# Sums of exponentials by TensorE for two pairs of heads, and division of the values in place of the probabilities

## The chip, the cores and the metric

The kernel runs on one core of one Trainium2 chip. The metric is the device time of one execution in microseconds (us); 742.13 us is the median of three runs of the kernel before (741.7 to 743.33).

## What is computed

Attention over 4 batches, 8 heads, 768 positions and 64 columns a head, with a window of 96 keys, 8 global keys and a bias by distance, and then a gated projection of its 3072 rows.

```python
scores = q @ k.T / 8 + bias          # kept: own window of 96 keys, and the first 8
a = exp(scores - max(scores))
a = a / (sum(a) + 1e-9)
x = (a @ v), heads side by side      # 3072 x 512
out = ((x @ w_a) * (x @ w_b)) @ w_out   # 512 -> 1536 -> 512
```

All inputs are float32. The weights arrive as 64-bit words and are rebuilt as float32 in the kernel.

## The kernel before

The 24 blocks of 128 query rows are cut into eight units, of 4, 2 and six times 3 blocks (`UNITS`). The first unit's attention runs ahead; then, unit by unit, its projection (`moe`) runs beside the attention of the next one. A projection has twelve steps (`f`), each with 128 of the 1536 columns: two products of 512-row contraction into the banks p0 and p1 (`proj`, L984), their product on ScalarE and VectorE (`raw`, L415 and L1023), a split of it into a high and a low part (`hh`, `hl`), and three products for each block into `acc` (`back`, L1002). Every factor is split so (`xh`, `xl` and the halves of `wt`), three products for one. During the first unit's projection the weights are converted by ScalarE and VectorE (`load_w`, L451 to L425).

The first unit (`first`) handles heads in four pairs, c = 0 to 3. A pair has two quads, j = 0 and 1, each of two blocks (`quad`): scores of both heads (`scores`, L783, into the banks `ps`), and for each head and block one window of 128, 256 or 232 columns. `softmax` subtracts the bias and takes the minimum of the negated scores on VectorE (L613), takes the exponential on ScalarE with the sum in an accumulator that is read by an instruction of its own (L629), adds 1e-9 (L644), takes the reciprocal (L651), and multiplies the window by it on VectorE, GpSimd or ScalarE (L661, L663). `turn` transposes the probabilities on TensorE into one of the banks `pt` (L688) and copies them to `pf` (L415, L417). `values` multiplies them with v into the bank `pa` (L736): the first head of the pair into its partitions 0 to 63, the second into 64 to 127, in turn. Then `pa` is cast to `xh` and the rest goes to `xl` (L843).

Each engine's order is written out by a planner (`Schedule.order`): every operation has a due time, a cost on each engine that may do it, and its buffers; an engine takes the ready operation that is due first. `search` tries 400 sets of jittered due times for the operations of the first two units' time and keeps the one with the earliest end. So a change of any operation there can move every other one. On the chip an engine then works through its list in that order and waits for semaphores. The queue of the SyncE engine (SP) issues all loads in its own order.

Of the kernel before, what the change touches and what calls it, by code (L numbers as in the profile page):

```python
# [13 lines left out]
F32 = mybir.dt.float32  # L14
# [11 lines left out]
P = 128  # L26
# [5 lines left out]
G = 8  # L32
# [6 lines left out]

CHUNKS = 12  # L40
SQ = 32

SHORT = PAIRED
OLD = (0, 2, 3)
# [329 lines left out]
class Fast:  # L374
    def __init__(self, ctx, tc, qkv, wts, out, raw0, consts):
        self.tc, self.nc = tc, tc.nc
        self.qkv, self.wts, self.out = qkv, wts, out
        rel, col, self.sc, self.ident = consts
        self.ctx = ctx
        self.w = {}  # L380
        self.plan = Schedule()
        self.negd = self.plan.buf(None, None, F32, "negd", "negd", tile=rel)
        self.negd0 = self.plan.buf(None, None, F32, "negd0", "negd0", tile=col)


        self.raw0 = self.plan.buf(None, None, F32, "raw0", "raw0", tile=raw0)
# [216 lines left out]
            )  # L603
        return qh, ql, kk

    def softmax(self, h, due, wins, ps, t, sm, done=()):

        nc, op, n = self.nc, self.plan.op, len(wins)
        for j, (o, w) in enumerate(wins):
            neg = self.negd if w > P else self.negd0  # L610
            op(
                due,
                lambda e, j=j, o=o, w=w, neg=neg: nc.vector.tensor_tensor_reduce(  # L613
                    t[:, o : o + w],
                    ps[:, o : o + w],
                    neg[:, :w],
                    -(2.0 ** -(h + 1)),
                    3.0e38,
                    ALU.add,
                    ALU.min,  # L620
                    sm[:, j : j + 1],
                ),
                [ps, neg, *done],
                [(t, j), (sm, j)],
                dve=dve(w) + 10,
            )
# [29 lines left out]
        for j, (o, w) in enumerate(wins):  # L656

            def norm(e, j=j, o=o, w=w):
                r = sm[:, 3 * n + j : 3 * n + j + 1]
                if e == "act":  # L660
                    nc.scalar.mul(t[:, o : o + w], t[:, o : o + w], r)  # L661
                else:
                    self.engine(e).tensor_scalar(  # L663
                        t[:, o : o + w], t[:, o : o + w], r, 1.0, op0=ALU.mult, op1=ALU.mult
                    )

            op(
                due,
                norm,
                [(sm, "r")],  # L670
                [(t, j)],
                port=BOTH,
                dve=130 + 0.52 * w,
                pool=243 + 0.836 * w,
                act=act(w) + 100,
            )
# [45 lines left out]
                    dma=SWAP,  # L722
                )

    def values(self, due, pl, blocks, v, probs, pa):


        nc = self.nc

        def emit(e):  # L730
            for i in blocks:
                slots = pl.vslot[i]
                for c, slot in enumerate(slots):
# [12 lines left out]
        self.plan.op(due, emit, reads, [pa], pe=n * 218 + 290, spare=SPARE if pl.late else 0.0)  # L746

    def quad(self, u, c, j, due, raw, v, pa, homes):


        nc, pl, op, sp = self.nc, PLANS[u], self.plan.op, self.sbuf
# [41 lines left out]
        for s in range(2):  # L793
# [5 lines left out]
            self.softmax(2 * c + s, due, wins, ps[s], t, sm)  # L799
            pt = self.bank(pick("pt"), f"pt{s}_{n}")  # L800
            pf = t
            if homes["pf"]:
# [7 lines left out]
                o += len(pl.vslot[i]) * P  # L810
        if pa is None:
            pa = self.bank("psS", f"pa{n}")
        self.values(due, pl, blocks, v, probs, pa)
        return pa

    def first(self, end):
# [7 lines left out]
        homes = {  # L824
            "q": ("hl", WIDE),
            "s": (("psS", "acc0"), ("p0", "acc2")),
            "pt": ("psT", "p1", "acc1"),
            "t": (("kk", MAXK), ("raw", MAXC)),
            "pf": (("hh", WIDE), ("v", 2 * MAXV * D)),
        }  # L830
        loads = [self.fetch_first(c, -1e6 + 2 * c) for c in range(NCC)]
        step = end / NCC
        for c in range(NCC):
            pa = self.bank("psA", f"pa0_{c}")
            for j in range(2):
                self.quad(0, c, j, c * step + (j + 1) * step / 2, *loads[c], pa, homes)
# [4 lines left out]
            self.plan.op(  # L841
                due,
                lambda e, lo=get(lo, l0), hi=get(hi, h0), pa=get(pa): self.nc.vector.tensor_sub(  # L843
                    lo(), pa(), hi()
                ),
                [pa, (hi, c)],
                [(lo, -c - 1)],
                dve=dve(WIDE),
            )
        return xh, xl  # L850
# [495 lines left out]
    return sc  # L1346


def build_first(nc, cp, qkv, sc):

    pl = PLANS[0]
# [10 lines left out]
def build(nc, a, out):  # L1362
    with tile.TileContext(nc) as tc, ExitStack() as ctx:
        cp = ctx.enter_context(tc.tile_pool(name="c", bufs=1))
        with tc.manual_schedule(), tc.tile_pool(name="tmp", bufs=1) as tp:
# [7 lines left out]
            raw0 = build_first(nc, cp, a["qkv"], sc)  # L1373
            ident = cp.tile([P, P], F32, name="ident")
            make_identity(nc, ident)
            nf = build_counts(nc, cp, nv)
# [4 lines left out]
        main = Fast(inner, tc, a["qkv"], a["wts"], out, raw0, (rel, col, sc, ident))  # L1381
        with tc.If(fast > 0) as branch:
            with inner:
                main.run()
# [75 lines left out]
```

## Time and profile before

| | |
|---|---|
| profiled execution | 742.13 us, span of the trace 740.2 us |
| median of three runs | 742.13 us |
| TensorE (PE) busy | 717.2 us, 97% |
| VectorE (DVE) busy | 458.0 us, 62% |
| ScalarE (ACT) busy | 394.9 us, 53% |
| GpSimd (POOL) busy | 10.5 us, 1% |

The shares are means over a start, in which attention of the first unit runs alone, and a long rest, in which TensorE works on projections all the time. The chain that ended last passes through TensorE for 93% of the span. Times of an instruction overlap with those of its successor on the same engine, so what one costs its engine is read from start to start.

### The profile page before, as it was taken

To read this page: it belongs to the slowest core of one execution; us is meant where nothing else is said; L and a number is where in the kernel's file an instruction comes from. 1 tells how busy PE (TensorE), PEld (TensorE's weight loads), DVE (VectorE), ACT (ScalarE), POOL (GpSimd) and SP (SyncE) were. 2 spreads that over 40 slices of the span, in tenths; PEclk is the share of its full clock that TensorE was granted. 3 is DMA by queue.
4 is the path that set the end of the run, shared out by engine and by line. 5 is a ranking of instruction groups with operands and counts; after the bars stand their busy time and mean duration, and the time that the engine had idled before them with its cause. 6 is when DMAs were issued, how large, how long until landed. Compare 5 with 4: busy or idle time off the path is not lost.

```text
span 740.2 us, 12564 instructions
## 1 busy us (share of the span) xinstructions
PE 717.2 (97%) x4374; PEld 642.7 (87%) x4374; DVE 458.0 (62%) x1479; ACT 394.9 (53%) x984; POOL 10.5 (1%) x30
## 2 busy tenths in 40 slices
PE   5789999999999999999999999999999999999996
PEld 3567777789988999999999999999999999989995
DVE  6999999957646765376635776167653776321111
ACT  6999866557655554265635556155553656321112
POOL 1000000000000000000000001000000000000000
PEclk9999999999999999999999999999999999999999
DMA  7889111112322334223331243323242242210001
GB/s 282 321 335 366 64 32 32 49 67 80 88 85 88 90 100 106 67 66 99 87 111 65 79 128 99 82 69 104 78 121 66 78 121 61 57 49 1 0 1 47
DMA packets 36215, 72.61 MB, mean 98 GB/s; under 512 B 7728, under 2 KB 18736, under 8 KB 36144
## 3 DMA queue, kind: packets, MB, share of 16 engines
q1 hardware_dynamic: 36144, 71.73, 30.8%
q8 instruction: 36, 0.59, 0.3%
q14 instruction: 35, 0.29, 0.1%
HBM read 50.07 MB, written 6.29 MB: 76 GB/s over the span
## 4 chain that ended last, share of the span: by engine, by line
PE 93%; ACT 3%; DVE 3%; DMA 0%; issue 0%; ACTq 0%
PE p L984 54%; PE acc L1002 27%; PE pa L736 5%; PE ps L909 4%; PE pt L688 1%; PE ps L783 1%; ACT t L629 1%; ACT wr L494 1%; ACT pf L415 1%; DVE t L613 0%; DMA nv<-ns 0%; ACT wm L457 0%; DVE kk L425 0%; ACT t L661 0%; DVE t L663 0%
## 5 line engine op out<-in xcount | busy, mean ns | idle before, releaser
L984 PE MATMUL p<-xh,wt 128*128 128x384 f32 (+2 forms) x1488 | 421.1, 339 | 3.5 <-ACT raw L415 1.9
L984 PEld LDWEIGHTS p<-xh,wt 128*128 128x128 f32 x1488 | 271.8, 189 | 17.8 <-issue 3.7
L984 PE MATMUL p<-xl,wt 128*128 128x384 f32 (+2 forms) x816 | 270.2, 341 | 1.2 <-ACT xl L415 0.9
L1002 PE MATMUL acc<-wt,hh 128*128 128x512 f32 x576 | 203.4, 395 | 0.6 <-ACT hh L415 0.6
L984 PEld LDWEIGHTS p<-xl,wt 128*128 128x128 f32 x816 | 153.8, 189 | 10.5 <-ACT xl L415 1.2
L1023 DVE TENSOR_TENSOR raw<-p,raw 128x384 f32<-128x384 f32 (+2 forms) x96 | 53.2, 555 | 156.0 <-PE p L984 133.0
L1002 PEld LDWEIGHTS acc<-wt,hh 128*128 128x128 f32 x576 | 108.2, 188 | 21.4 <-issue 1.1
L1002 PE MATMUL acc<-wt,hl 128*128 128x512 f32 x288 | 113.2, 393 | 0.4 <-DVE hl L425 0.4
L415 ACT COPY raw<-p 128x384 f32<-128x384 f32 (+2 forms) x96 | 45.8, 477 | 114.0 <-PE p L984 113.7
L415 ACT CAST hh<-raw 128x384 fp32r<-128x384 f32 (+2 forms) x84 | 43.2, 514 | 49.6 <-DVE raw L1023 48.7
L425 DVE TENSOR_TENSOR hl<-raw,hh 128x384 fp32r<-128x384 f32 (+2 forms) x96 | 53.3, 556 | 24.8 <-ACT hh L415 24.2
L629 ACT ACTIVATE t<-t,sm 128x232 f32<-128x232 f32 (+2 forms) x120 | 56.9, 477 | 17.1 <-DVE sm L613 16.1
L1002 PEld LDWEIGHTS acc<-wt,hl 128*128 128x128 f32 x288 | 54.2, 188 | 8.3 <-DVE hl L425 0.7
L613 DVE CUSTOM_DVE_ANT_0 t<-ps,rel 128x232 f32<-128x232 f32 (+1 forms) x100 | 39.1, 400 | 28.2 <-PE ps L909 27.1
L661 ACT ACTIVATE t<-t,sm 128x232 f32<-128x232 f32 (+2 forms) x77 | 36.1, 479 | 18.7 <-DVE sm L651 14.9
L629 ACT ACTIVATE wm<-wm,sm 128x232 f32<-128x232 f32 (+2 forms) x72 | 34.1, 474 | 19.1 <-DVE sm L613 18.4
L661 ACT ACTIVATE wm<-wm,sm 128x232 f32<-128x232 f32 (+2 forms) x66 | 31.3, 478 | 21.0 <-DVE sm L651 13.6
L736 PE MATMUL pa<-pf,v 128*64 128x128 f32 x640 | 41.8, 277 | 0.6 <-PE pt L688 0.4
L736 PEld LDWEIGHTS pa<-pf,v 128*64 128x64 f32 x640 | 34.4, 137 | 8.4 <-issue 6.6
L425 DVE TENSOR_TENSOR kk<-raw,kk 64x244 fp32r<-64x244 f32 (+1 forms) x86 | 39.9, 464 | 2.6
L909 PE MATMUL ps<-kk,ql 128*128 128x128 f32 (+1 forms) x144 | 39.4, 275 | 0.0
L909 PE MATMUL ps<-kk,qh 128*128 128x128 f32 (+1 forms) x144 | 38.1, 267 | 0.0
(89 smaller groups left out, 666.7 us busy)
## 6 DMA issues: line engine op xcount, KB each, us to landing
wr<-wts SPq DMA_DIRECT2D x24, 768.0 KB, 12.0
pf<-wm SPq DMA_DIRECT2D x192, 48.0 KB, 1.9
raw<-qkv SPq DMA_DIRECT2D x24, 366.0 KB, 3.1
raw<-qkv SPq DMA_DIRECT2D x24, 314.0 KB, 2.9
v<-qkv SPq DMA_DIRECT2D x16, 384.0 KB, 3.5
out<-o SPq DMA_DIRECT2D x23, 256.0 KB, 2.1
pf<-wm SPq DMA_DIRECT2D x144, 40.0 KB, 1.9
v<-qkv SPq DMA_DIRECT2D x16, 256.0 KB, 2.8
```

Source lines behind the costliest of these rows:

```text
L415: self.nc.scalar.copy(out(), src())
L425: lambda e: self.engine(e).tensor_sub(out(), a(), b()),
L494: lambda e, low=low: nc.scalar.activation(low(), low().bitcast(U32), AF.Copy, scale=2.0**-29),
L613: lambda e, j=j, o=o, w=w, neg=neg: nc.vector.tensor_tensor_reduce(t[:, o : o + w], ps[:, o : o + w], neg[:, :w], -(2.0 ** -(h + 1)), 3.0e ...
L629: lambda e, j=j, o=o, w=w: nc.scalar.activation(t[:, o : o + w], t[:, o : o + w], AF.Exp, bias=sm[:, j : j + 1], scale=-1.0, accum_out=sm[ ...
L661: nc.scalar.mul(t[:, o : o + w], t[:, o : o + w], r)
L688: nc.tensor.transpose(pt[:, c * P : c * P + P], t[:, o : o + P], self.ident)
L736: nc.tensor.matmul(pa[D * s : D * s + D, i * P : i * P + P], v[:, v0 : v0 + D], probs[s, i][1](c), start=c == 0, stop=c == len(slots) - 1,)
L909: nc.tensor.matmul(ps[:, :w], q[:, i * P : i * P + P], kk[:, k0 : k0 + w], start=m == 0, stop=m == 1,)
L984: nc.tensor.matmul(p[:, :T], wt(), b[:, b0 : b0 + T], start=c == 0 and n == 0, stop=c == NCC - 1 and n == 2,)
L1002: nc.tensor.matmul(acc[i][:, :], hs[:, i * P : i * P + P], wt(), start=f == 0 and n == 0, stop=f == NF - 1 and n == 2,)
L1023: lambda e, asb=asb, pb=pb: nc.vector.tensor_mul(asb[:, :T], pb[:, :T], asb[:, :T]),
```

## The change

For the pairs c = 0 and 1 of the first unit (`SUMS`), `softmax` stops behind the exponential, which no longer has an accumulator. `values` gives TensorE, behind each product of v and probabilities, one of a matrix of ones (or of zeros and ones, where a slot holds fewer than 128 keys) and the same probabilities, into the same partitions of a bank `su`: every one of the 64 rows of a head gets the sums. ScalarE copies the sums plus 1e-9 to `y`, VectorE takes the reciprocal of all 512 columns and multiplies `pa` by it, and `xh` and `xl` are made of `y`. `su` lies in the bank acc1, which the transposed probabilities used as their third. GpSimd builds the matrix of ones at the start.

```diff
+SUMS = (0, 1)
-    def softmax(self, h, due, wins, ps, t, sm, done=()):
+    def softmax(self, h, due, wins, ps, t, sm, done=(), norm=True):
...
-                    accum_out=sm[:, n + j : n + j + 1],
+                    **({"accum_out": sm[:, n + j : n + j + 1]} if norm else {}),
...
-                act=act(w) + 200,
+                act=act(w) + (200 if norm else 100),
+        if not norm:
+            return
...
-    def values(self, due, pl, blocks, v, probs, pa):
+    def values(self, due, pl, blocks, v, probs, pa, sums=None):
...
+                        if sums:
+                            keys = len(pl.vkeys[slot][1])
+                            nc.tensor.matmul(
+                                sums[D * s : D * s + D, i * P : i * P + P],
+                                self.ones[:, :D] if keys == P else self.ones[:, D:],
+                                probs[s, i][1](c),
+                                start=c == 0,
+                                stop=c == len(slots) - 1,
+                            )
...
+        out = [pa, sums] if sums else [pa]
+        cost = len(out) * n * 218 + 290
...
-            "pt": ("psT", "p1", "acc1"),
+            "pt": ("psT", "p1"),
...
+            if c in SUMS:
+                sums = self.bank("acc1", f"su0_{c}")
...
+            y = pa
+            if sums:
+                y = sp([P, CHUNKS * P], F32, "pf", f"y0_{c}")
...
+                    lambda e, y=get(y), sums=get(sums): self.nc.scalar.activation(
+                        y(), sums(), AF.Identity, bias=self.tiny[:, 0:1]
+                    ),
...
+                    lambda e, y=get(y): self.nc.vector.reciprocal(y(), y()),
...
+                    lambda e, y=get(y), pa=get(pa): self.nc.vector.tensor_mul(y(), pa(), y()),
...
-            self.copy(due, get(hi, h0), get(pa), WIDE, [pa], [(hi, c)], psum=True)
+            self.copy(due, get(hi, h0), get(y), WIDE, [y], [(hi, c)], psum=sums is None)
...
-                    lo(), pa(), hi()
+                    lo(), y(), hi()
...
+def build_ones(nc, cp):
+    ones = cp.tile([P, 2 * D], F32, name="ones")
+    nc.gpsimd.iota(
+        ones, [[0, 2 * D]], base=0, channel_multiplier=1, allow_small_or_imprecise_dtypes=True
+    )
+    nc.gpsimd.tensor_scalar(ones, ones, float(P - LW - G), 0.0, op0=ALU.is_ge, op1=ALU.add)
+    nc.gpsimd.memset(ones[:, :D], 1.0)
+    tiny = cp.tile([P, 1], F32, name="tiny")
+    nc.gpsimd.memset(tiny, 1e-9)
```

The lists change with it. In names as `ps1_0_0_1` the first digit is the head of the pair, then unit, pair and quad. TensorE behind the first pair's scores, before:

```order
L688 MATMUL pt1_0_0_0_193<-ident_93,t1_0_0_0_162 128x128 x3
L688 MATMUL pt0_0_0_0_200<-ident_93,t0_0_0_0_157 128x128 x3
L783 MATMUL ps0_0_1_0_214<-raw0_1_160,qs0_1_0_207 128x128
L783 MATMUL ps1_0_1_0_216<-raw0_1_160,qs0_1_0_207 128x128
L783 MATMUL ps0_0_1_0_214<-raw0_1_160,qs0_1_0_207 128x256
L783 MATMUL ps1_0_1_0_216<-raw0_1_160,qs0_1_0_207 128x256
L688 MATMUL pt1_0_0_1_227<-ident_93,t1_0_0_1_173 128x128 x4
L783 MATMUL ps0_0_1_1_238<-raw0_1_160,qs0_1_1_222 128x232
```

and now, behind three transposes and the first two slots of values (L800 is the old L783, L693 the old L688, L742 the old L736, L751 the ones):

```order
L742 MATMUL pa0_0_210<-pf0_0_0_0_191,v0_0_155 64x128
L751 MATMUL su0_0_212<-pf0_0_0_0_191,ones_98 64x128
L742 MATMUL pa0_0_210<-pf1_0_0_0_207,v0_0_155 64x128
L751 MATMUL su0_0_212<-pf1_0_0_0_207,ones_98 64x128
L693 MATMUL pt1_0_0_1_232<-ident_93,t1_0_0_1_185 128x128 x4
L800 MATMUL ps0_0_1_0_239<-raw0_1_166,qs0_1_0_226 128x128
L800 MATMUL ps1_0_1_0_241<-raw0_1_166,qs0_1_0_226 128x128
L800 MATMUL ps0_0_1_0_239<-raw0_1_166,qs0_1_0_226 128x256
L800 MATMUL ps1_0_1_0_241<-raw0_1_166,qs0_1_0_226 128x256
L800 MATMUL ps0_0_1_1_247<-raw0_1_166,qs0_1_1_228 128x232
```

The values of the first quad, which stood behind the third pair's scores, now stand ahead of the second pair's, and each has a product with ones behind it.

VectorE where the second pair's windows end, before (L613 is a window with its minimum, with a row for the read of the minimum; L768 scales queries):

```order
L651 RECIPROCAL sm0_0_1_0_233<-sm0_0_1_0_233 128x2
L613 ISA t0_0_1_1_270,sm0_0_1_1_271<-ps0_0_1_1_238,rel_70 128x232
L613 ISA sm0_0_1_1_271 128x1
L663 TENSOR_SCALAR t0_0_1_0_232<-t0_0_1_0_232,sm0_0_1_0_233 128x256
L613 ISA t1_0_1_1_274,sm1_0_1_1_275<-ps1_0_1_1_240,rel_70 128x232
L613 ISA sm1_0_1_1_275 128x1
L644 TENSOR_SCALAR sm1_0_1_0_236<-sm1_0_1_0_236 128x2
L768 TENSOR_SCALAR qs0_3_0_289<-raw0_3_212,sc_79 128x256
L651 RECIPROCAL sm1_0_1_0_236<-sm1_0_1_0_236 128x2
L663 TENSOR_SCALAR t1_0_1_0_235<-t1_0_1_0_235,sm1_0_1_0_236 128x128
```

and now (L616 is the old L613, L785 the old L768, L873 the reciprocal and L881 the multiplication of `y`, L419 a cast):

```order
L785 TENSOR_SCALAR qs0_2_1_297<-raw0_2_200,sc_79 128x256
L873 RECIPROCAL y0_0_304<-y0_0_304 128x512
L616 ISA t0_0_2_0_330,sm0_0_2_0_331<-ps0_0_2_0_310,col_71 128x128
L616 ISA sm0_0_2_0_331 128x1
L881 TENSOR_TENSOR y0_0_304<-pa0_0_210,y0_0_304 128x512
L616 ISA t0_0_2_0_330,sm0_0_2_0_331<-ps0_0_2_0_310,rel_70 128x256
L616 ISA sm0_0_2_0_331 128x1
L419 CAST xh0_345<-y0_0_304 128x512
L616 ISA t1_0_2_0_363,sm1_0_2_0_364<-ps1_0_2_0_312,col_71 128x128
L616 ISA sm1_0_2_0_364 128x1
L616 ISA t1_0_2_0_363,sm1_0_2_0_364<-ps1_0_2_0_312,rel_70 128x256
```

The small adds and reciprocals and the normalizations are gone; the reciprocal of 512 columns stands ahead of the third pair's first window, and the multiplication and the cast of `y` between its windows.

ScalarE up to the copy of the first projection out of its bank, before (L494 and L457 convert weights):

```order
L494 ACTIVATE wr2_0_434<-wr2_0_434 128x768
L494 ACTIVATE wr2_1_459<-wr2_1_459 128x768
L457 ACTIVATE wm_440<-wr2_0_434 128x768
L415 CAST xl0_387<-pa0_3_592 128x512
L494 ACTIVATE wr3_0_488<-wr3_0_488 128x768
L494 ACTIVATE wr3_1_510<-wr3_1_510 128x768
L415 CAST wt1_0_654<-wm_440 128x768
L494 ACTIVATE wr4_1_557<-wr4_1_557 128x768
L415 COPY raw0_88<-p00_0_535 128x512
```

and now (L496, L459 and L417 are the old L494, L457 and L415):

```order
L417 COPY pf0_0_3_1_613<-pt0_0_3_1_603 128x512
L496 ACTIVATE wr1_1_366<-wr1_1_366 128x768
L496 ACTIVATE wr2_0_427<-wr2_0_427 128x768
L417 CAST wt1_0_638<-wm_398 128x768
L417 CAST xl0_370<-pa0_3_553 128x512
L459 ACTIVATE wm_398<-wr2_0_427 128x768
L496 ACTIVATE wr2_1_456<-wr2_1_456 128x768
L459 ACTIVATE wm_398<-wr2_1_456 128x768
L417 COPY raw0_88<-p00_0_572 128x512
```

Fewer weight conversions stand ahead of the copy (the last row of each), and those of the third step in another order.

## Rows read from the trace of the kernel before

**Rows 1.** The page's head and its busy time of each engine
```profile
span 740.2 us, 12564 instructions
...
PE 717.2 (97%) x4374; PEld 642.7 (87%) x4374; DVE 458.0 (62%) x1479; ACT 394.9 (53%) x984; POOL 10.5 (1%) x30
```

**Rows 2.** Stretches: busy us (instructions) of PE, PEld, DVE, ACT, POOL, TensorE clock, DMA
```profile
17.40:50.10 32.70, 25.34 (x214) 18.32 (x210) 31.93 (x111) 32.16 (x83) 0.00 (x0) 0.95 0.83 316
50.10:100.00 49.90, 49.87 (x250) 39.37 (x251) 49.70 (x96) 45.19 (x80) 0.00 (x0) 1.00 0.56 215
```

**Rows 3.** The chain of waits: start us, us, what
```profile
49.61 0.47 ACT raw L415
...
50.13 1.90 PE p L984 x7
```

**Rows 4.** Timeline, ScalarE: start us, us, instruction, [idle before <-releaser]
```profile
7.79 0.40 ACT L629 ACTIVATE t<-t,sm 128x128 f32<-128x128 f32 x1 [1.65 <-DVE sm L613]
...
18.23 0.47 ACT L629 ACTIVATE t<-t,sm 128x232 f32<-128x232 f32 x1
18.61 0.19 ACT L629 ACTIVATION_READ_ACCUMULATOR t<-t,sm 128x1 f32 x1
18.70 0.47 ACT L629 ACTIVATE t<-t,sm 128x232 f32<-128x232 f32 x1
...
22.57 0.58 ACT L415 CAST xh<-pa 128x512 fp32r<-128x512 f32 x1
23.04 1.09 ACT L415 COPY pf<-pt 128x512 f32<-128x512 f32 x2
```

**Rows 5.** Timeline, VectorE, 17 to 24 us
```profile
17.28 0.16 DVE L644 TENSOR_SCALAR sm<-sm 128x2 f32<-128x2 f32 x1
17.35 0.39 DVE L613 CUSTOM_DVE_ANT_0 t<-ps,rel 128x232 f32<-128x232 f32 x1
...
18.05 0.35 DVE L663 TENSOR_SCALAR t<-t,sm 128x256 f32<-128x256 f32 x1
18.31 0.39 DVE L613 CUSTOM_DVE_ANT_0 t<-ps,rel 128x232 f32<-128x232 f32 x1
...
20.51 0.16 DVE L651 RECIPROCAL sm<-sm 128x2 f32<-128x2 f32 x1
20.59 0.40 DVE L613 CUSTOM_DVE_ANT_0 t<-ps,rel 128x256 f32<-128x256 f32 x1
...
23.37 0.69 DVE L843 TENSOR_TENSOR xl<-pa,xh 128x512 fp32r<-128x512 f32 x1
23.97 0.39 DVE L613 CUSTOM_DVE_ANT_0 t<-ps,rel 128x232 f32<-128x232 f32 x1
```

**Rows 6.** Groups of VectorE instructions by shape: busy us, mean ns, idle before
```profile
L651 DVE RECIPROCAL sm<-sm 128x1 f32<-128x1 f32 x144 | 23.2, 161 | 3.9
...
L651 DVE RECIPROCAL sm<-sm 128x2 f32<-128x2 f32 x24 | 3.8, 160 | 0.1
```

**Rows 7.** Timeline, TensorE, the first 22 us
```profile
5.80 3.20 PE L783 MATMUL ps<-raw 64*128 64x128 f32 x16 [5.80 <-DVE rel L1335]
...
12.51 1.66 PE L783 MATMUL ps<-raw,qs 64*128 64x128 f32 x8
...
20.31 1.75 PE L736 MATMUL pa<-pf,v 128*64 128x128 f32 x28
21.99 1.42 PE L688 MATMUL pt<-ident,t 128*128 128x128 f32 x11
```

**Rows 8.** Stretches of 0.05 us, TensorE's instructions on pa: busy us (in flight), clock, DMA
```profile
20.30:20.35 0.05, 0.04 (x2) 1.00 1.46 614
...
20.45:20.50 0.05, 0.05 (x4) 1.00 0.58 246
```

**Rows 9.** Timeline, VectorE, at the sixth step
```profile
85.88 0.95 DVE L425 TENSOR_TENSOR wt<-wm,wt 128x768 fp32r<-128x768 f32 x1
```

**Rows 10.** Timeline, TensorE, at the sixth step
```profile
87.47 0.39 PE L984 MATMUL p<-xh,wt 128*128 128x512 f32 x1
```

More of the change, by code (lines that the diff above doesn't have):

```diff
@@ L377, in __init__ @@
         self.qkv, self.wts, self.out = qkv, wts, out
-        rel, col, self.sc, self.ident = consts
+        rel, col, self.sc, self.ident, self.ones, self.tiny = consts
         self.ctx = ctx
@@ L742, in emit, with quad @@
                         )
+                        if sums:
[7 more added lines that the diff above has]
+                            )
         reads = [v] + [probs[s, i][0] for s in range(2) for i in blocks]
         n = sum(len(pl.vslot[i]) for i in blocks)
-        self.plan.op(due, emit, reads, [pa], pe=n * 218 + 290, spare=SPARE if pl.late else 0.0)
-    def quad(self, u, c, j, due, raw, v, pa, homes):
+        out = [pa, sums] if sums else [pa]
+        cost = len(out) * n * 218 + 290
+        self.plan.op(due, emit, reads, out, pe=cost, spare=SPARE if pl.late else 0.0)
+    def quad(self, u, c, j, due, raw, v, pa, homes, sums=None):
         nc, pl, op, sp = self.nc, PLANS[u], self.plan.op, self.sbuf
@@ L798, in quad @@
             sm = sp([P, 8], F32, "sm", f"sm{s}_{n}", 6)
-            self.softmax(2 * c + s, due, wins, ps[s], t, sm)
+            self.softmax(2 * c + s, due, wins, ps[s], t, sm, norm=sums is None)
             pt = self.bank(pick("pt"), f"pt{s}_{n}")
@@ L812, in quad @@
             pa = self.bank("psS", f"pa{n}")
-        self.values(due, pl, blocks, v, probs, pa)
+        self.values(due, pl, blocks, v, probs, pa, sums)
         return pa
@@ L833, in first @@
         for c in range(NCC):
-            pa = self.bank("psA", f"pa0_{c}")
+            pa, sums = self.bank("psA", f"pa0_{c}"), None
+            if c in SUMS:
+                sums = self.bank("acc1", f"su0_{c}")
             for j in range(2):
-                self.quad(0, c, j, c * step + (j + 1) * step / 2, *loads[c], pa, homes)
+                self.quad(0, c, j, c * step + (j + 1) * step / 2, *loads[c], pa, homes, sums)
             (hi, h0), (lo, l0) = xh[c], xl[c]
@@ L839, in first @@
             due = (c + 1) * step
-            self.copy(due, get(hi, h0), get(pa), WIDE, [pa], [(hi, c)], psum=True)
+            y = pa
+            if sums:
+                y = sp([P, CHUNKS * P], F32, "pf", f"y0_{c}")
+                self.plan.op(
+                    due,
+                    lambda e, y=get(y), sums=get(sums): self.nc.scalar.activation(
+                        y(), sums(), AF.Identity, bias=self.tiny[:, 0:1]
+                    ),
+                    [sums],
+                    [y],
+                    act=act(WIDE, True),
+                )
+                self.plan.op(
+                    due,
+                    lambda e, y=get(y): self.nc.vector.reciprocal(y(), y()),
+                    [],
+                    [y],
+                    port=BOTH,
+                    dve=dve(WIDE),
+                )
+                self.plan.op(
+                    due,
+                    lambda e, y=get(y), pa=get(pa): self.nc.vector.tensor_mul(y(), pa(), y()),
+                    [pa],
+                    [y],
+                    dve=dve(WIDE),
+                )
+            self.copy(due, get(hi, h0), get(y), WIDE, [y], [(hi, c)], psum=sums is None)
             self.plan.op(
                 due,
-                lambda e, lo=get(lo, l0), hi=get(hi, h0), pa=get(pa): self.nc.vector.tensor_sub(
-                    lo(), pa(), hi()
+                lambda e, lo=get(lo, l0), hi=get(hi, h0), y=get(y): self.nc.vector.tensor_sub(
+                    lo(), y(), hi()
                 ),
-                [pa, (hi, c)],
+                [y, (hi, c)],
                 [(lo, -c - 1)],
+                port=BOTH if sums else (),
                 dve=dve(WIDE),
@@ L1346, in build_scales @@
     return sc
+def build_ones(nc, cp):
+    ones = cp.tile([P, 2 * D], F32, name="ones")
+    nc.gpsimd.iota(
+        ones, [[0, 2 * D]], base=0, channel_multiplier=1, allow_small_or_imprecise_dtypes=True
+    )
+    nc.gpsimd.tensor_scalar(ones, ones, float(P - LW - G), 0.0, op0=ALU.is_ge, op1=ALU.add)
+    nc.gpsimd.memset(ones[:, :D], 1.0)
+    tiny = cp.tile([P, 1], F32, name="tiny")
+    nc.gpsimd.memset(tiny, 1e-9)
+    return ones, tiny
 def build_first(nc, cp, qkv, sc):
@@ L1375, in build @@
             make_identity(nc, ident)
+            ones, tiny = build_ones(nc, cp)
             nf = build_counts(nc, cp, nv)
@@ L1380, in build @@
         inner = ctx.enter_context(ExitStack())
-        main = Fast(inner, tc, a["qkv"], a["wts"], out, raw0, (rel, col, sc, ident))
+        main = Fast(inner, tc, a["qkv"], a["wts"], out, raw0, (rel, col, sc, ident, ones, tiny))
         with tc.If(fast > 0) as branch:
```

## The prediction

> **What bounds the kernel now.** First the page's head and busy shares: TensorE is busy for 717.2 of 740.2 us, so the time is its work plus the little it stands still [rows 1]. Next the stretches: from 50.1 us on it hardly stands (49.87 of 49.90 us); what it loses, it loses ahead of that. In 17.4 to 50.1 VectorE is busy for 31.93 and ScalarE for 32.16 of 32.70 us, TensorE for 25.34 [rows 2]. I call the moment when TensorE begins the second of the twelve steps of the first projection the handover. The chain of waits shows what sets it: ScalarE works without a break through casts and weight conversions, copies the first projection out of its bank at 49.61, and TensorE begins at 50.13 [rows 3]. Ahead of the handover both programs give TensorE the same projection work (24 products of 512 columns), and behind it the same remainder. So the change is worth what it moves the handover, less what TensorE must wait behind it.
>
> **ScalarE up to that copy.** An exponential of 232 columns takes 0.38 us until its accumulator is read and 0.09 more until the next begins (18.23, 18.61, 18.70) [rows 4]; the change drops sixteen reads: 16 x 0.09 = 1.44. Two normalizations of the first two pairs stood here, of 232 and 128 columns: the 0.38 of such a pass and some 0.3, together 0.7. Added are two copies of sums at the 0.47 of a 512-column pass (22.57 to 23.04) [rows 4]: 0.94. The new order also moves work: a cast of x (0.47) and a copy of probabilities (0.36) go to VectorE, three scalings of queries come here (3 x 0.4), normalizations of later pairs cost 0.5 more, and two more weight conversions of 0.8 fall behind the copy. Sum: -1.44 - 0.7 + 0.94 - 0.83 + 1.2 + 0.5 - 1.6 = -1.9.
>
> **VectorE up to the last subtraction of x.** Removed: 8 adds and 8 reciprocals at 0.07 to 0.08, 1.2, and 14 normalizations, 0.26 for 256 columns (18.05 to 18.31) and a little less for the ten smaller ones, 3.4 [rows 5]. Added: two multiplications of 512 columns at the 0.60 of a subtraction of that size (23.37 to 23.97), 1.2 [rows 5], and two reciprocals of 512 columns, which no row shows. Their low end is the same 0.60. The high end comes from the small ones: a successor begins 0.08 behind a reciprocal (20.51, 20.59) and 0.07 behind an add (17.28, 17.35) [rows 5]; were that 0.01 the price of two columns, 5 ns each, 512 would cost 0.60 + 2.6 = 3.2. I take 0.60: 144 reciprocals of one column average 161 ns and 24 of two columns 160, so that the second column costs nothing visible [rows 6]. The moves add 0.8 (cast, copy) and take away 0.8 of query scalings and some normalizations, one of them to GpSimd. Sum about -3.4. The subtraction for these pairs reads SBUF now, at the same 0.60.
>
> The Trainium skill, "VectorE: DVE Perf Modes", section "First, the fixed hardware budget", says that Reciprocal runs an iterative divide with a repeat count of 8. If that is eight cycles a column at the page's 0.96 GHz, each would take 4.3 us, an estimate, and the sum above would go from -3.4 to +4. The rows of one and two columns [rows 6] speak against it, but are too short to refuse it.
>
> **TensorE ahead of the handover.** 28 products with ones are added: of the two operations that form a pair's values, 12 rows become 24 and 16 become 32 (a product is two rows). Now 28 rows take 20.31 to 21.99, 0.12 us a product [rows 7], and the rows in flight come in twos (2, then 4) [rows 8]: the two heads of a pair run beside each other, each in half of the array's columns. The added products alternate otherwise, values and ones of one head, then of the other, so equal halves meet. Low end: they pair as well, and the operations take 24 and 32 times 0.06, 1.5 and 2.0 us, instead of 0.7 and 1.0. High end: nothing overlaps, twice that. I take the low end: a product that waits for its half lets the next one, of the other half, start beside it, so the loss is one product at the front of each operation.
>
> The Trainium skill, "TensorE: Matmul & The Clock Gate", section "Part 3: Packing small matmuls", says that matmuls start and end strictly in program order. Held to the single rows of a product, that makes six slots where four would do, as in the first rival below. The starts in twos [rows 8] fit it only if the two heads are interleaved row by row.
>
> **The start.** Without the wait for sums, transposes follow the exponentials at once, but the first values with ones now stand ahead of the second pair's scores. Scores of the first pair end at 9.0 as before [rows 7]. ScalarE's eight exponentials and two copies end at 11.8; TensorE runs values from 11.1 to 12.6, a transpose, and the second pair's scores from 13.1, where they began at 12.51 [rows 7]. But both halves follow each other now, so VectorE ends that pair's eight windows at 16.5; the last of them began at 18.31 [rows 5]. The copy of sums follows the second values at 17.2, the reciprocal runs 17.8 to 18.4. ScalarE stands still for about 1.1 (the transpose behind the first values), 0.7 (between exponentials, and for the sums) and 0.4 (a later transpose), 2.2 in all. Now it is 3.1: from the first exponential at 7.79 [rows 4] there are 39.1 of work, and the copy is over at 50.0. So then it is over at 7.79 + 37.2 + 2.2 = 47.2, and the handover comes 2.9 earlier. VectorE's last subtraction ends near 45.5, ahead of that.
>
> GpSimd's four added small instructions stand ahead of the branch, where TensorE's first product waits until 5.80 anyhow [rows 7]: nothing. Should they outlast that cover, each 0.1 is lost outright. The sums take the third bank of transposed probabilities; the copies out of the other two come 0.2 late once, which costs nothing behind the wait for the first values. Of the loads ahead of the weights only the order changes, with the first pair's values now first, in time for 11.1.
>
> **Behind the handover.** At the sixth step the low half of the weights is ready at 85.88 + 0.95 = 86.83 [rows 9], and TensorE begins it at 87.47 [rows 10]: a lead of 0.6, and VectorE is busy for 49.70 of 49.90 us there [rows 2]. Moved up by 2.9, TensorE eats into such leads, while the work of VectorE ahead of each step's product is less by 0.8 to 5.7, least at the fourth. I count two short waits, 0.5 together. Sum: -2.9 + 0.5 = -2.4.
>
> **Time.** The profiled execution took 742.13, 740.2 of it in the span and 1.9 around; the median of the runs shown is the same 742.13. Forecast 742.13 - 2.4 = 739.7; its own range is 738.7 to 740.9.
>
> **Rivals.**
> *Ones that do not pair.* At six slots for four, TensorE's four operations take 0.6 and 0.75 us longer each, 2.7 in all, and the second pair's scores, both copies of sums and all behind them on ScalarE wait for that. For it: equal halves meet, and the chain of the start runs through these operations twice a pair. Against: the starts in twos [rows 8]. Some 0.4 is idle time anyway: 739.7 + 2.3 = 742.0. With no overlap at all, as much again: 744.
>
> *Reciprocal by the column.* Place: VectorE, between the third pair's windows and again ahead of the fourth's. It decides from about 2 us each. At 3.2 it is 2 x 2.6 = 5.2, of which idle time of VectorE takes 0.8: 739.7 + 4.4 = 744.1, slower. For it: its length is unseen. Against: [rows 6]. By the page's eight cycles, as an estimate, it would be 2 x 3.7 - 0.8 = 6.6 and 746.3.
>
> *Given back.* The handover moves, but weights come no earlier: TensorE waits at the third to sixth steps until the old spacing is reached, 2.4 more: 742.1. For it: the lead of 0.6 and a full VectorE. Against: VectorE has 3.4 less to do.
>
> **How the numbers follow.** Forecast 0.50, ones 0.17, reciprocal 0.22, given back 0.11. Within 0.2% (1.5 us) a measurement of this kernel can hardly tell a change from none. The forecast's range is faster but for its edge, and a few of the milder "ones" are too: 0.53. Most of the "ones" and all of "given back" are no change, 0.22; the reciprocal and the ones at their worst are slower, 0.25. The range 738.6 to 744.8 takes in the ones at their worst and the reciprocal at the rows' bound, and leaves out the page's estimate and a better start.
>
> **What would show it.** Right: the second projection step begins near 47.2, the last copy ahead of it is ScalarE's, reciprocals of 512 columns take 0.6 to 0.7, 24 and 32 rows 1.5 and 2.0, and TensorE is idle for under 1 us from there to 150. Wrong: reciprocals over 2 us with ScalarE waiting for the third pair's windows; values with ones at 2.1 and 2.75 us; waits of TensorE for weights between 55 and 100.

## The result

The changed kernel takes 744.75 us (median of 17 runs) against 742.13 for the kernel before (17 runs): ratio 1.0034, 95% interval 1.0025 to 1.0043. It is slower by 2.6 us; the prediction was 739.7, faster. The profiled execution has a span of 743.6, which answers to [rows 1], and TensorE has the 56 added rows (4374 before, 4430 now):

```profile
span 743.6 us, 12639 instructions
...
PE 723.0 (97%) x4430; PEld 647.3 (87%) x4430; DVE 459.3 (62%) x1448; ACT 396.1 (53%) x971; POOL 14.7 (2%) x36
```

The stretches that answer to [rows 2] are the first and the last row; three short ones lie between (busy us of PE, PEld, DVE, ACT, POOL, then TensorE's clock and DMA):

```profile
17.40:54.20 36.80, 29.23 (x216) 20.60 (x213) 34.18 (x90) 30.80 (x75) 0.47 (x1) 0.86 0.74 283
20.00:21.00 1.00, 0.00 (x0) 0.00 (x0) 1.00 (x1) 0.00 (x0) 0.00 (x0) 1.00 0.98 406
23.00:24.00 1.00, 1.00 (x14) 1.00 (x13) 1.00 (x6) 1.00 (x6) 0.00 (x0) 0.50 1.01 418
33.00:34.00 1.00, 0.00 (x0) 0.00 (x0) 1.00 (x5) 0.00 (x0) 0.00 (x0) 0.50 0.15 61
54.20:100.00 45.80, 45.79 (x229) 36.38 (x230) 45.65 (x90) 42.28 (x75) 0.00 (x0) 1.00 0.58 228
```

The handover stands at 54.21 (last row of TensorE below), where it was 50.13 [rows 3]: 4.1 later, where 2.9 earlier was forecast. What lies behind it is 743.6 - 54.21 = 689.4, against 740.2 - 50.13 = 690.1: nothing is lost there, 0.7 is gained. What is lost lies in the first row: ScalarE is busy for 30.80 of 36.80 us, where it was 32.16 of 32.70. At 20 to 21 and at 33 to 34 VectorE is the only engine at work. TensorE is granted 0.50, the lower of its two clock levels (1.2 of 2.4 GHz), at 23 to 24, behind a wait of 2.26 us, and at 33 to 34, within one of 2.42 (both below). The kernel before has a stretch at that level too, without any wide reciprocal, after 3 us in which TensorE was busy for 1.3; it is part of the 0.95 of [rows 2]:

```profile
36.00:39.00 3.00, 2.94 (x7) 2.36 (x8) 3.00 (x12) 3.00 (x10) 0.00 (x0) 0.50 1.04 427
```

VectorE's timeline shows what it does in the changed kernel:

```profile
16.73 0.08 DVE L616 DVE_READ_ACCUMULATOR2_ANT sm<- 128x1 f32 x1
...
18.06 3.35 DVE L873 RECIPROCAL y<-y 128x512 f32<-128x512 f32 x1 [0.98 <-ACT y L864]
21.33 0.23 DVE L616 CUSTOM_DVE_ANT_0 t<-ps,col 128x128 f32<-128x128 f32 x1
...
29.83 3.34 DVE L873 RECIPROCAL y<-y 128x512 f32<-128x512 f32 x1
...
33.11 0.41 DVE L616 CUSTOM_DVE_ANT_0 t<-ps,rel 128x256 f32<-128x256 f32 x1
...
33.45 0.69 DVE L881 TENSOR_TENSOR y<-pa,y 128x512 f32<-128x512 f32 x1
```

The 512-column reciprocals (L873) take 3.35 and 3.34 us; from start to start, as the forecast's terms are, the first costs VectorE 3.27. Everything up to the first stands where the forecast had it: the last window at 16.73 (forecast 16.5), the reciprocal at 18.06 (17.8). Behind it waits a window of the third pair (L616, 21.33), and behind the second the windows of the fourth (33.11) and the product (33.45). ScalarE waits behind both:

```profile
17.36 0.67 ACT L864 ACTIVATE y<-su,tiny 128x512 f32<-128x512 f32 x1
...
21.66 0.40 ACT L632 ACTIVATE t<-t,sm 128x128 f32<-128x128 f32 x1 [2.10 <-DVE sm L616]
...
25.90 0.59 ACT L417 COPY pf<-pt 128x512 f32<-128x512 f32 x1 [1.12 <-PE pt L693]
...
34.17 0.62 ACT L417 CAST xh<-y 128x512 fp32r<-128x512 f32 x1 [2.11 <-DVE y L881]
...
36.82 0.59 ACT L417 COPY pf<-pt 128x512 f32<-128x512 f32 x1 [0.66 <-PE pt L693]
...
53.58 0.58 ACT L417 COPY raw<-p 128x512 f32<-128x512 f32 x1
```

It stands for 2.10 ahead of 21.66, for a window, and for 2.11 ahead of 34.17, for the product; twice more it stands for transposes, 1.12 ahead of 25.90 and 0.66 ahead of 36.82. That is 6.0 in all. The last row is the copy that sets the handover. TensorE:

```profile
11.18 0.45 PE L742 MATMUL pa<-pf,v 128*64 128x128 f32 x4
11.45 0.39 PE L751 MATMUL su<-pf,ones 128*64 128x128 f32 x4
11.67 0.44 PE L742 MATMUL pa<-pf,v 128*64 128x128 f32 x4
...
12.69 0.66 PE L693 MATMUL pt<-ident,t 128*128 128x128 f32 x4
13.28 1.71 PE L800 MATMUL ps<-raw,qs 64*128 64x128 f32 x16
14.92 0.45 PE L742 MATMUL pa<-pf,v 128*64 128x128 f32 x4
...
16.86 0.87 PE L693 MATMUL pt<-ident,t 128*128 128x128 f32 x6
...
22.23 0.45 PE L742 MATMUL pa<-pf,v 128*64 128x128 f32 x4 [2.26 <-DVE y L881]
...
24.75 1.12 PE L693 MATMUL pt<-ident,t 128*128 128x128 f32 x4
...
34.19 1.55 PE L742 MATMUL pa<-pf,v 128*64 128x128 f32 x12 [2.42 <-DVE y L881]
...
54.21 0.50 PE L1031 MATMUL p<-xh,wt 128*128 128x512 f32 x1
```

The first three lines are part of the operation that forms the first pair's values; its 24 rows run from 11.18 to 12.69, the 32 of the next from 14.92 to 16.86. Twice TensorE stands for VectorE's product (2.26 and 2.42), which has to free the bank `pa`. The second pair's 24 rows then take 22.23 to 24.75, 2.5 us where the first pair's took 1.5, most of it at the lower clock level, and the transposes for which ScalarE waits at 25.90 stand behind them.

### The profile page after: what moved, and what is told of

It reads as the page before. It is cut to its first block, busy times and chain, and to the rows that moved or that the text cites. A ratio compares the mean times of both kernels' runs of the same rounds, so it can differ in the third digit from the quotient of the medians.

```text
span 743.6 us, 12639 instructions
## 1 busy us (share of the span) xinstructions
PE 723.0 (97%) x4430; PEld 647.3 (87%) x4430; DVE 459.3 (62%) x1448; ACT 396.1 (53%) x971; POOL 14.7 (2%) x36
## 4 chain that ended last, share of the span: by engine, by line
PE 94%; DVE 2%; ACT 2%; issue 1%; DMA 0%; ACTq 0%; DVEq 0%
PE p L1031 55%; PE acc L1049 27%; PE pa L742 6%; PE ps L956 4%; PE pt L693 1%; PE ps L800 1%; ACT t L632 1%; DVE y L873 0%; DVE t L616 0%; DMA nv<-ns 0%; ACT wr L496 0%; PE su L751 0%; ACT pf L417 0%; ACT wm L459 0%; DVE y L881 0%
## 5 line engine op out<-in xcount | busy, mean ns | idle before, releaser
L417 ACT COPY raw<-p 128x384 f32<-128x384 f32 (+2 forms) x96 | 45.7, 476 | 105.9 <-PE p L1031 104.4
L417 ACT CAST hh<-raw 128x384 fp32r<-128x384 f32 (+2 forms) x88 | 45.0, 511 | 47.1 <-DVE raw L1070 47.0
L632 ACT ACTIVATE t<-t,sm 128x232 f32<-128x232 f32 (+2 forms) x120 | 55.7, 472 | 17.8 <-DVE sm L616 17.1
L616 DVE CUSTOM_DVE_ANT_0 t<-ps,rel 128x232 f32<-128x232 f32 (+1 forms) x100 | 38.8, 399 | 25.0 <-PE ps L956 23.3
L742 PE MATMUL pa<-pf,v 128*64 128x128 f32 x640 | 47.4, 286 | 5.9 <-DVE y L881 4.7
L742 PEld LDWEIGHTS pa<-pf,v 128*64 128x64 f32 x640 | 37.3, 141 | 14.7 <-issue 6.9
L666 ACT ACTIVATE t<-t,sm 128x232 f32<-128x232 f32 (+2 forms) x72 | 33.8, 482 | 20.0 <-DVE sm L656 15.6
L427 DVE TENSOR_TENSOR kk<-raw,kk 64x348 fp32r<-64x348 f32 (+1 forms) x85 | 39.4, 464 | 2.6
```

The source lines that it names most:

```text
L417: self.nc.scalar.copy(out(), src())
L427: lambda e: self.engine(e).tensor_sub(out(), a(), b()),
L632: lambda e, j=j, o=o, w=w: nc.scalar.activation(t[:, o : o + w], t[:, o : o + w], AF.Exp, bias=sm[:, j : j + 1], scale=-1.0, **({"accum_ou ...
L742: nc.tensor.matmul(pa[D * s : D * s + D, i * P : i * P + P], v[:, v0 : v0 + D], probs[s, i][1](c), start=c == 0, stop=c == len(slots) - 1,)
```

## The experiments

The ratios are to the kernel before on the same chip, whose median there was 741.9 to 742.7; so a difference between the times of two rows is good to some 0.8 us. "Handover" and "behind", the span less the handover, are of the one profiled execution. "Behind" lies between 687.5 and 691.3, so the handover tells where a large difference comes from, and not a small one.

| run | time, us | ratio to before, 95% | handover | behind |
|---|---|---|---|---|
| after | 744.75 | 1.0025 to 1.0043 | 54.21 | 689.4 |
| 1 product for reciprocal | 738.92 | 0.9932 to 0.9966 | 47.87 | 689.2 |
| 2 no sums, two banks | 742.08 | 0.9984 to 1.0008 | 51.11 | 689.7 |
| 3 before plus reciprocals | 753.13 | 1.0110 to 1.0166 | 58.68 | 691.3 |
| 4 halves | 745.07 | 1.0026 to 1.0053 | 55.38 | 687.5 |
| 5 first product only | 740.98 | 0.9978 to 0.9998 | 50.17 | 689.0 |
| 6 planner told | 741.75 | 0.9991 to 1.0013 | 51.88 | 687.7 |
| 7 compact sums | 750.58 | 1.0098 to 1.0133 | 60.99 | 687.8 |
| 9 other draw | 745.71 | 1.0032 to 1.0072 | 53.82 | 690.1 |
| 10 told, other draw | 746.03 | 1.0044 to 1.0078 | | |
| 11 compact, 64 columns | 738.10 | 0.9940 to 0.9973 | 48.09 | 687.9 |
| 12 compact, ones apart | 737.85 | 0.9933 to 0.9965 | 47.87 | 688.0 |
| 13 bank freed early | 744.31 | 1.0019 to 1.0041 | 53.69 | 689.6 |
| 14 compact, other draw | 739.93 | 0.9968 to 0.9988 | 50.68 | 689.4 |

In run 10 TensorE goes into the second step without a wait, and the handover is not read there. The profiled execution of run 14 took 741.9, so that its handover is later than that of the median would be.

**1. A product in place of the reciprocal.** Order and queues stay, only the price changes.

```diff
-lambda e, y=get(y): self.nc.vector.reciprocal(y(), y()),
+lambda e, y=get(y): self.nc.vector.tensor_mul(y(), y(), y()),
```

> The changed kernel with both 512-column reciprocals replaced by a product of y with itself (tensor by tensor, same place, same queues, same order); the division is left out of the arithmetic. Theory A (the loss is the price of the two reciprocals, 3.35 us each where 0.6 was forecast): each product takes 0.6 to 0.7, the handover comes back from 54.2 to 47.5 to 49.5, and the time is 738.5 to 741, 4 to 6 below the changed kernel and 1 to 3.5 below the kernel before. Rival B (TensorE's 56 added rows and its lower clock): the handover stays at 53 to 54 and the time at 743.5 to 745.5. Rival C (the new order and the bank taken from the transposes): the same 743.5 to 745.5.

The first of VectorE's two products, TensorE at the handover and two stretches, of this run:

```profile
18.42 0.69 DVE L873 TENSOR_TENSOR y<-y 128x512 f32<-128x512 f32 x1 [0.98 <-ACT y L864]
```

```profile
47.87 0.50 PE L1031 MATMUL p<-xh,wt 128*128 128x512 f32 x1
```

```profile
20.00:30.00 10.00, 9.31 (x107) 6.99 (x104) 9.69 (x42) 10.00 (x30) 0.46 (x1) 1.00 1.02 418
30.00:40.00 10.00, 6.96 (x45) 4.22 (x45) 9.87 (x33) 10.00 (x28) 0.00 (x0) 1.00 0.77 297
```

The handover comes back by 6.3 us, to 47.87, the time to 738.92, 5.8 below the changed kernel. The ones' products and the new order are all still there, so rivals B and C fall. ScalarE is full again, and TensorE's clock is at its full level from 20 to 40: its fall in the changed kernel followed the waits.

**2. No sums, two banks.**

```diff
-SUMS = (0, 1)
+SUMS = ()
```

> The changed kernel with SUMS empty: no products with ones, no 512-column reciprocals, every probability divided as before; what is left of the change is the transposes' two banks in place of three and the order that the planner makes of that. Theory A: the time of the kernel before, 741 to 743. Rival C (bank and order): 743.5 to 746, the loss is there without any reciprocal. Rival B says 741 to 743 as well.

742.08, the kernel before: giving up the transposes' third bank, and the order that the planner makes of that, cost nothing that can be measured.

**3. The reciprocals in the kernel before.**

```diff
+ c < 2 and self.nc.vector.reciprocal(lo(), pa()),
  self.nc.vector.tensor_sub(lo(), pa(), hi()),
```

> The kernel before, in its own order, with one reciprocal of 512 columns (from pa into lo, overwritten by the subtraction right behind it) issued ahead of VectorE's subtraction of the first and of the second pair; the result is that of before. Theory A: 3.3 us each on VectorE, whose next windows and divisions wait; the handover moves from 50.1 to between 53 and 56.8 and the time is 745 to 748.5, 3 to 6.5 above before. Rivals B and C (VectorE has room for 6.7 us): within 0.5 of before, 741.7 to 742.7.

The direction of theory A, but 10.4 us (753.13 against 742.71 on that chip) instead of 3 to 6.5. The reciprocals' group, two waits of ScalarE, and a stretch behind them:

```profile
L844 DVE RECIPROCAL xl<-pa 128x512 fp32r<-128x512 f32 x2 | 6.7, 3354 | 0.0
```

```profile
27.41 0.49 ACT L629 ACTIVATE t<-t,sm 128x232 f32<-128x232 f32 x1 [2.81 <-DVE sm L613]
...
40.44 0.59 ACT L415 CAST xh<-pa 128x512 fp32r<-128x512 f32 x1 [4.31 <-PE pa L736]
```

```profile
36.00:48.00 12.00, 9.52 (x43) 7.16 (x44) 11.65 (x34) 7.69 (x21) 0.00 (x0) 0.50 0.39 145
```

VectorE's 6.7 us leave ScalarE standing for 2.81 and 4.31, and TensorE goes on for 12 us at its lower clock level (0.50). So the price alone slows a kernel that has nothing else of the change; that the lower clock makes up the excess is read from these rows and was not tested apart.

**4. Two halves.** Copy, reciprocal and product go to halves of 256 columns, with 1700 as the planner's price of each half.

> The changed kernel with copy, reciprocal and product in two halves of 256 columns, each as soon as its two query blocks have their sums, and with the planner told 1.70 us for each half. Theory A (by the column): each half takes about 1.7; the first half of the first pair falls into VectorE's empty stretch around 13 to 16.8, so about 1.7 us of the 6.7 leave the path: 741 to 743.5, 1 to 3 below the changed kernel. If the price were by the instruction, each half would take 3.3 and the time would be 747 or more. Rivals B and C: 744 to 745.

The two VectorE rows that decide it:

```profile
13.45 1.75 DVE L876 RECIPROCAL y<-y 128x256 f32<-128x256 f32 x1 [2.26 <-ACT y L867]
...
17.01 0.42 DVE L884 TENSOR_TENSOR y<-pa,y 128x256 f32<-128x256 f32 x1 [1.52 <-PE su L751]
```

The price is by the column, 1.75 for 256. But nothing is gained (745.07): the order made from this puts the first half's product ahead of all but one of the second pair's windows, where it waits 1.52 for the sums' later products, so VectorE stands in the stretch that was to be filled. This run tells the price, not what hiding it would bring.

**5. Only the first pair's reciprocal replaced.**

```diff
+ self.nc.vector.reciprocal(y(), y())
+ if c
+ else self.nc.vector.tensor_mul(y(), y(), y())
```

> The changed kernel with the reciprocal of the first pair alone replaced by a product of y with itself (0.69 us in the last such run); that of the second pair stays at 3.35; the division of the first pair is left out of the arithmetic. Theory A, both reciprocals stand on the path that sets the handover and their prices add: about half of the 5.8 us that both cost, 741 to 742.5, handover near 51. Rival D, only one of the two does (the first delays the windows of the third pair behind it, the second is behind everything that the handover needs, or the other way round): 739 to 740 or 744 to 745.

740.98, just below theory A's range, handover 50.17. Both reciprocals stand on the path: the first is worth 3.8 us (744.75 to 740.98; 4.0 at the handover) and the second 2.1 (to 738.92; 2.3), against 2.66 less on VectorE for each. Rival D falls. All waits of ScalarE from 17 to 50 (total us, times, longest):

```profile
ACT xh L417 <- DVE y L885: 2.1, 1, 2.1
```

Of the changed kernel's four waits the one for the second product is left. With the first reciprocal went the 2.10 for a window and also the 1.12 and 0.66 for transposes, 3.9 in all; so it costs more than its own 2.66 by delaying TensorE as well. What the bank and the lower clock level each contribute to these two waits was not tested apart.

**6, 9, 10. What the order is worth.** The planner priced a reciprocal at about 602. Run 6 gives it 3350, run 9 another seed of its search, run 10 both.

```diff
-dve=dve(WIDE),
+dve=3350.0,
...
-rnd = random.Random(1)
+rnd = random.Random(2)
```

> The changed kernel with 3350 in place of about 602 as the planner's price of each 512-column reciprocal; the order is made anew from it, the work is the same. If the wrong price in the planner was what failed, the order works around the reciprocals and 741.5 to 743.5 comes out, 1 to 3 below the changed kernel. If VectorE has no room for them in any order: 744 to 746.

> The changed kernel, its arithmetic and its prices, with another seed for the planner's search of due times: another order of the same work. If the loss comes from the reciprocals' price wherever the order puts them at 0.60: 743.5 to 746, as the changed kernel. If one order or another is worth as much as the planner's right price gained (3.0 us): 741 to 743.

> The planner told 3350 for each 512-column reciprocal, as in the run before with that price, and the other seed. If the right price is what gained: 741 to 743 again. If the gain was the luck of one order: 743.5 to 746.

Told the price, the planner finds 741.75 with one seed and 746.03 with the other; not told, 744.75 and 745.71. One seed would have been read as "the wrong price was the failing". With two, the same work with the same prices differs by 4.3 us from draw to draw (a draw is the order that one seed gives), and what the right price is worth stays open. The kernel before was run with one seed only; the nearest to a second draw of it is run 2, at 742.08. Runs 1, 3, 5 and 13 keep an order and are free of this.

**8. The price by width.** SUMS is empty, and a chain of reciprocals stands in the prologue (its one time, 745.39, has 3.06 us of them and a wait ahead of the branch and is not used).

> SUMS empty, and in the prologue reciprocals of 1, 2, 4, 8, 16, 32, 64 and 128 columns on 128 partitions in a scratch tile, one after another. Theory A, a price by the column throughout (3.35 at 512 and 1.75 at 256 give 6.25 ns a column and 0.15 beside): 0.16 for 1 and 2, 0.20 for 8, 0.35 for 32, 0.55 for 64 and 0.95 for 128. Rival: flat up to some width, then the slope.

Its groups by shape (busy us, mean ns of one, idle before):

```profile
L1439 DVE RECIPROCAL ones<-ones 128x128 f32<-128x128 f32 x1 | 1.0, 953 | 0.0
L1439 DVE RECIPROCAL ones<-ones 128x64 f32<-128x64 f32 x1 | 0.6, 553 | 0.0
...
L1439 DVE RECIPROCAL ones<-ones 128x2 f32<-128x2 f32 x1 | 0.2, 166 | 0.0
L1439 DVE RECIPROCAL ones<-ones 128x1 f32<-128x1 f32 x1 | 0.2, 163 | 2.5 <-POOL tiny L1406 2.5
```

A straight line: 6.25 ns a column from 64 to 128 ((953 - 553) / 64), and on to the 1.75 and 3.35 of 256 and 512, with 0.15 beside it. From one column to two it is 163 to 166 ns.

**7, 11, 12, 14. Cheaper sums.** The changed kernel writes each sum on 64 partitions. These versions write it on 32, two query blocks beside each other, so that a pair's sums lie on 256 columns; VectorE inverts those out of PSUM, four products with a selecting matrix spread them again (into the bank of the sums), and ScalarE copies pa meanwhile. They leave out the 1e-9.

```diff
+ sums[SQ * (2 * (i % 2) + s) :, i // 2 * P : i // 2 * P + P][:SQ],
+ self.ones[:, :SQ] if keys == P else self.ones[:, D : D + SQ],
...
+ self.nc.vector.reciprocal(y[:, r], sums[:, : 2 * P])
+ self.nc.scalar.copy(y(), pa())
+ self.nc.tensor.matmul(sums[:, o : o + P], self.sel[:, k * P : k * P + P],
+     y[:, WIDE + j * P : WIDE + j * P + P], start=True, stop=True)
+ self.nc.vector.tensor_mul(y[:, k], y[:, k], sums[:, o])
```

> A version with cheaper divisions: the products with ones write 32 rows for each head and query block, two blocks' heads side by side on the partitions, so that the sums of a pair lie on 256 columns in place of 512; VectorE takes the reciprocal of these straight from PSUM; four products with a matrix that picks one row of each 32 spread it again over 64 rows a head; ScalarE copies pa meanwhile, and VectorE multiplies. By the column (theory A): 1.75 for each reciprocal in place of 3.35; two products of 0.42 in place of one of 0.69; 1.45 less on VectorE for each pair; from 738.9 (with 0.69 in place of a reciprocal) about 1.2 more for each pair: 740 to 742, below the kernel before if the added steps (VectorE to TensorE to VectorE) hide. Rival: the longer chain of steps and the order made anew give it back: 742.5 to 745.

Run 7 missed by far, 750.58. TensorE's timeline, and its two groups up to 60 us:

```profile
12.06 0.41 PE L751 MATMUL su<-pf,ones 128*32 128x128 f32 x2
12.39 0.43 PE L742 MATMUL pa<-pf,v 128*64 128x128 f32 x2
12.76 0.41 PE L751 MATMUL su<-pf,ones 128*32 128x128 f32 x2
```

```profile
L742 PE MATMUL pa<-pf,v 128*64 128x128 f32 x112 | 17.5, 292 | 2.8 <-ACT pf L417 2.8
L751 PE MATMUL su<-pf,ones 128*32 128x128 f32 x56 | 11.4, 285 | 0.0
```

Values (64 columns) and ones (32) alternate, and now each head's product runs alone, 0.33 to 0.36 us, where the changed kernel runs both heads' in 0.22 (11.45 to 11.67 above). This is the rival "ones that do not pair", in a kernel where it does happen. Two ways out: 64 columns half of which are zeros (11), or all values ahead of all ones (12).

> The compact sums with a stationary matrix of 64 columns, half of them zeros, in place of 32 columns: two query blocks' sums add into one 64-row region, so that every product of the values and of the ones has the same 64 columns. Theory E, heads' products run beside each other only where the tile keeps its shape from one to the next: groups of four rows every 0.22 us as in the changed kernel, TensorE's part of 17.5 and 11.4 us falls back to about 13 and 7, and with reciprocals of 1.75 the time is 739.5 to 742. Rival: the chain of steps from VectorE to TensorE and back is the loss, 745 or more.

> The compact sums with 32 columns, but with all products of the values of an operation ahead of all products with ones, so that the shape changes once and not at every product. Theory E: both kinds run two heads at a time, TensorE's part falls as with 64 columns, 739.5 to 742.5. Rival (a product of 32 columns never runs beside another): values pair, ones don't, 743 to 747.

The ones' group in run 11, both groups in run 12, then TensorE in run 12, with a stretch of its products with ones (busy us, rows in flight, clock, DMA):

```profile
L752 PE MATMUL su<-pf,ones 128*64 128x128 f32 x56 | 6.0, 273 | 0.0
```

```profile
L742 PE MATMUL pa<-pf,v 128*64 128x128 f32 x112 | 9.4, 281 | 2.8 <-ACT pf L417 2.8
...
L754 PE MATMUL su<-pf,ones 128*32 128x128 f32 x56 | 2.6, 280 | 0.0
```

```profile
11.16 0.88 PE L742 MATMUL pa<-pf,v 128*64 128x128 f32 x12
11.97 0.64 PE L754 MATMUL su<-pf,ones 128*32 128x128 f32 x12
```

```profile
11.95:12.00 0.05, 0.03 (x4) 1.00 0.94 394
```

Both are as theory E has it, and a little better than its ranges. In run 12 the 32-column products take 0.048 us a row (12 rows in 11.97 to 12.54), less than the 0.068 of the values before them (12 rows in 0.81): their first four begin together, where rows of 64 columns begin in twos. 737.85 is 4.1 us below the kernel before and 6.9 below the changed one. Run 14 is run 12 with the other seed:

> The fastest version so far (sums on 256 columns, values ahead of ones, 737.85) with the other seed of the planner's search, the same work in another order. If its 4 us below the kernel before come from the cheaper work: 737 to 739.5. If they were the luck of one order, as in the run where the planner was told the reciprocal's price: 740 to 743.

739.93 lies between the two ranges. With either seed this work beats the kernel before, but what it gains is 4.1 us with one draw and 1.9 with the other.

**13. By which way the price reaches the handover.** TensorE's waits of 2.26 and 2.42 are for the bank of pa, which is free only behind the product. Order and reciprocals stay, ScalarE copies pa at once:

```diff
+ self.nc.scalar.activation(y[:, WIDE : 2 * WIDE], sums(), AF.Identity, bias=...),
+ self.nc.scalar.copy(y[:, :WIDE], pa()),
...
-lambda e, ...: self.nc.vector.tensor_mul(y(), pa(), y()),
+lambda e, ...: self.nc.vector.tensor_mul(y[:, :WIDE], y[:, :WIDE], y[:, WIDE : 2 * WIDE]),
```

> The changed kernel in its own order, with both 512-column reciprocals at 3.35; ScalarE copies pa into SBUF right behind the sums, and VectorE's product reads that copy. So TensorE's next values no longer wait for the bank of pa until the product behind the reciprocal is done; VectorE's queue is as before; ScalarE has two passes of some 0.5 more. Theory F, the reciprocal costs through the bank that it holds (TensorE stands 2.26 and 2.42 us for that product): those two waits go, the handover comes back by 2 to 5 and the time is 740 to 742.5. Theory G, it costs through VectorE's queue (the third and fourth pairs' windows stand behind it and ScalarE waits for them): the handover stays at 53 to 55 and the time is 744 to 746.

All waits of ScalarE in this run from 17 to 53 (total us, times, longest):

```profile
ACT t L632 <- DVE sm L616: 1.6, 1, 1.6
ACT xh L417 <- DVE y L886: 1.6, 1, 1.6
ACT y L865 <- PE su L751: 0.8, 1, 0.8
```

TensorE's two long waits are gone, and the time is 744.31 with the handover at 53.69: the numbers of theory G. ScalarE still waits for a window behind the first reciprocal, as G has it, and for the product behind the second, where the result itself is late and not a window. But this does not refute F in full: ScalarE stands for 4.0 us instead of 6.0, and the two copies that this version adds to its work (0.57 and 0.58) take back about one of these two. So most of the price goes by VectorE and a part, up to 2 us, by the bank; that part was not measured alone.

## Why the prediction was wrong

**The step that failed is the size of one term**, VectorE's "I take 0.60" for each 512-column reciprocal. It is 3.27 from start to start, so VectorE's sum of -3.4 becomes -3.4 + 2 x 2.67 = +1.9, on an engine with hardly a gap in the stretch. (Of that -3.4 the terms with a number give -2.2; the rest is "some normalizations" without one.) The working had the upper bound, 3.2 each from the 0.01 us by which a successor of a two-column reciprocal came later [rows 5], and put it aside for the means of 161 and 160 ns [rows 6]. That the bound came so near is luck, since 0.01 is the last digit of those rows. Run 8 shows what those means hide: a second column costs 3 ns of 163, too little to be seen in means over instructions with different neighbours. Equal times at widths where the fixed part is nearly all of the duration say nothing about a slope.

The Trainium skill ("VectorE: DVE Perf Modes", "First, the fixed hardware budget") gives a repeat count of 8; if that is eight cycles a column at its 0.96 GHz, the estimate is 8.3 ns a column. The rows of run 8 say 6.25, six such cycles. It named the right kind of cost, and the forecast should have weighed it above the short rows.

**The rival "Reciprocal by the column" is what happened**, ahead of the third and of the fourth pair's windows and at its price: 744.1 for 3.2 each, 744.75 measured at 3.35. It had 0.22. That the times agree so well is in part luck: it let idle time of VectorE take 0.8, and the two cost 5.8 (6.3 at the handover) against 5.3 less work, but it also began from 739.7, 0.8 too high. Run 1 confirms it from the other side, run 3 reproduces the loss in the kernel before. Runs 5 and 13 show the way: ScalarE stands for a window in VectorE's queue behind the first, for the result itself behind the second, and for TensorE, which waits for the same products.

**The rest of the working held, with errors of 0.7 and -1.3 that partly cancel.** With the term at its forecast size (run 1, 0.69) the time is 738.92, forecast 739.7. The handover is at 47.87, forecast 47.2: ScalarE and the start were 0.7 too early. Behind it the forecast lost 0.5; the runs gain 0.7 (changed kernel) and 0.8 (run 1), so "given back" did not happen. The start came in order: second pair's scores 13.28 (13.1), copy of sums 17.36 (17.2).

**TensorE's low end was right**: 1.5 and 1.9 us for 24 and 32 rows of the first pair (forecast 1.5 and 2.0), so "ones that do not pair" falls for this kernel. The reason given was an engine that lets the next product of the other half start; the rows go further. The program has values and ones of one head, then of the other, and the trace shows four rows of values, then four of ones: the heads' equal products meet across the one between them. The Trainium skill ("TensorE: Matmul & The Clock Gate", "Part 3: Packing small matmuls") has starts strictly in program order; these rows, in the order in which they are recorded, do not agree.

**Not foreseen** was that the waits also take TensorE's clock to its lower level, at 23 to 24 and 33 to 34 us. That it follows the waits is shown by run 1. How much of the 5.8 us it carries is open: of the 6.0 us for which ScalarE stands, 1.8 wait for TensorE's transposes, and it would show there beside the bank.

## What to carry to other kernels

Measure an unseen operation at the size at which it will run, or take its price from the upper bound, when all rows at hand are so short that their fixed part hides a slope. Here, moving a division from many narrow scalars to one wide tile gained only with the sums packed into fewer columns, and only where the products of two heads still ran beside each other (runs 11, 12 and 14, not 7); unpacked it gained in none of four orders; and when a planner draws the order, two draws are needed before a change of a few us is put down to the work.

## What the runs showed of the hardware

- A reciprocal on VectorE costs 6.25 ns a column and 0.15 us beside it (0.95 us at 128 columns, 3.35 at 512), where a product of 512 columns takes 0.69.
- Two heads' fp32 products in separate halves of the columns ran beside each other (four rows in 0.22 us) across a product of the same shape between them, but not where that one was 32 columns wide instead of 64 (0.33 to 0.36 us for each head's two rows); 32-column products among themselves ran at 0.048 us a row.
- TensorE was granted 0.50 of its clock (1.2 of 2.4 GHz) at 33 to 34 us of the changed kernel, where it stood for a 3.34 us instruction of VectorE, and 1.00 from 30 to 40 with products of 0.69 us in place of the reciprocals.
